# Twelve instead of sixteen weights prepared beside attention, eight converted in place in layer two, longer transfer lags in the plan, and the last product in two column halves

## The chip, the cores and the metric

One Trainium2 chip, one NeuronCore of it. The metric is the device time of one execution in microseconds (us). PE is TensorE, which multiplies; DVE is VectorE, ACT is ScalarE; POOL (GpSimd) and SP (SyncE) only issue transfers here. PSUM holds the products until ACT or DVE reads them.

## The reference

```python
scores = scale * np.matmul(q, k.transpose(0, 1, 3, 2))      # 2 batches, 12 heads, 448 tokens, 64 wide
scores = np.einsum('bhij,hg->bgij', scores, w_pre)          # mix the heads
scores = scores - np.max(scores, axis=-1, keepdims=True)
attn = np.exp(scores)
attn = attn / (np.sum(attn, axis=-1, keepdims=True) + 1e-09)
attn = np.einsum('bhij,hg->bgij', attn, w_post)             # mix them again
x = np.matmul(attn, v)                                      # -> 896 tokens x 768
h = x @ w_in;  g = h * (1.0 / (1.0 + np.exp(-1.702 * h)));  x = g @ w_out           # layer one, 768 -> 2048 -> 768
h = x @ w_in2                                                                       # layer two
P = a[0] + a[1]*h + a[2]*h*h + a[3]*h*h*h
Q = 1.0 + np.abs(b[0])*np.abs(h) + np.abs(b[1])*h*h
out = (P / (Q + 1e-06)) @ w_out2
```

The four weight matrices arrive as 64-bit words; the kernel turns each word into a 32-bit number with integer operations.

## The kernel before

**No loop sets the order.** Every piece of work is a `step` with the engines that may do it, an assumed duration, the steps it needs, a rank, and the buffers it takes and gives back. `Plan.issue` plays these steps through once while the program is built, with assumed hops between engines (`HOP`) and assumed transfer times (`DMA_LAG`, `RG_LAG`, `W_LAG`, `A_LAG`, `LD_LAG`, `ST_LAG`), and writes each engine's instructions in the order that comes out. On the chip each engine follows its list strictly and waits at each instruction for its inputs. Where a real transfer is later than assumed, the engine that needs it stands, with everything behind it in its list.

**Attention** runs over 8 chunks of query rows (4 to a batch). `scores` (L356, 6 pairs of heads to a chunk) multiplies q and k; ACT or DVE copy the pair into S; `regroup` (L392, issued by SP) sends rows of S into a tile T so that 10 query rows by 12 heads lie on 120 partitions; `pre` (L397) mixes heads; DVE takes the maximum, ACT the exponential; `post` (L446, and L449 for the last 64 keys) mixes again and turns the rows; `av` (L472) multiplies with v. There are 90 such groups; chunk 5 begins with group 57. While PE waits for the first loads, `fill` runs multiplications of a constant (L257).

**The layers.** A unit `up` (L715 to L717, 18 matmuls for one tile of 128 hidden columns and one half of 448 tokens) makes h; the activation runs on ACT and DVE; a unit `down` (L782 to L784, 12 matmuls to a half) multiplies four tiles back, and DVE adds its PSUM bank to `yt` (L271). `down` has two banks `mm`, `up` four banks `bk`. Weights and activations are split into a high and a low part, so each product takes three matmuls.

**A weight** (name: layer, u or d, number; `u` tiles 768 columns, `d` tiles 512) goes through: load of the raw words by POOL (`w_load`, L661, three `raw` buffers); ACT takes the magnitude (`wmag`, L666); DVE does four integer steps (`w_bits`, L671, L673, L675, L678); a copy gives the high part (`whi`), ACT writes its negative (`w_minus`, L700), and POOL issues an adding transfer that makes the low part (`w_part`, L692; in the plan `w`). In this kernel all 40 weights of layer two take a detour (`ahead`): they are converted early, stored to DRAM (`w_store`, L684) and fetched again (`w_fetch`, L688) when layer two needs them. The first `EARLY` = 16 of them are converted beside attention, the other 24 spread over layer one. POOL's list holds all these transfers in one row, so an adding transfer behind a load waits until that load's buffer is free.

Of the kernel before, what the change touches and what calls it, by code (L numbers as in the profile page):

```python
# [17 lines left out]
B, H, S, D = 2, 12, 448, 64  # L18
# [10 lines left out]
FQ = 4  # L29
DMA_LAG = 3500  # L30
RG_LAG = 5000
W_LAG = 4500

# [21 lines left out]
HOP |= {("pe", False): 280, ("pe", True): -80, ("pool", False): 85, ("pool", True): 100}  # L55
FILL_NS, FILL_WIN, FILL_MIN = 210, 2600, 0.55
NQ = NF // FQ
TB = 10
# [5 lines left out]
LATE = 2400, 1400, 1000  # L64
A_LAG = 5000
LD_LAG = 6500, 4500
ST_LAG = 8500, 4500
EARLY = 16
MID = 60
# [6 lines left out]
class Plan:  # L76
# [35 lines left out]
    def issue(self):  # L112
# [50 lines left out]
        while events and events[0][0] < 1e8:  # L163
# [15 lines left out]
            for e in idle:  # L179
# [23 lines left out]
                else:  # L203
                    dry.add(e)
                    if e == "pe" and self.fill and more:
                        b = next((b for b in ("bk", "mm") if self.pick(b) is not None), None)
                        if now >= self.fill_from and b and busy(now) < FILL_MIN * FILL_WIN:
                            mode = "f"
                            idle[e] = now + FILL_NS
                            runs.append((now, now + FILL_NS))  # L210
                            order.append((b, self.pick(b)))
                        heapq.heappush(events, (now + FILL_NS, 2, ()))
# [24 lines left out]
def talking_heads_then_two_ffn(ctx: ExitStack, tc: tile.TileContext, q, k, v, wpre, wpost, win1, wout1, win2, wout2, ab, out):  # L237
# [12 lines left out]
    def psum(b, *n):  # L250
        return banks[b][plan.bank[n, b]]
# [517 lines left out]

    def down(L, qq, m, halves):  # L770
        gt = t_["g", L, qq]
        p = psum("mm", "down", L, qq, m, halves)
        if m % 3 == 0:

            pe.matmul(p[:, halves[0], S:], warm[:, :128], warm[:, : 512 - S], start=True, stop=True)
        w = t_["w", (L, "d", qq * KK + m)]
        for hf in halves:
            t_["y", L, qq, m, hf] = p
            cs = slice(hf * S, hf * S + S)
            for i in range(FQ):  # L780
                ms = slice(i * 128, i * 128 + 128)
                pe.matmul(p[:, hf, :S], w[:, 0, ms], gt[:, 0, i, cs], start=i == 0, stop=False)  # L782
                pe.matmul(p[:, hf, :S], w[:, 1, ms], gt[:, 0, i, cs], start=False, stop=False)  # L783
                pe.matmul(p[:, hf, :S], w[:, 0, ms], gt[:, 1, i, cs], start=False, stop=i == FQ - 1)  # L784

    def down_out(L, qq, m, halves, eng):
        if ("yt", L) not in t_:
            t_["yt", L] = held("yt", "out", L, qq, m, halves)
        hs = slice(halves[0], halves[-1] + 1)
        o, p = t_["yt", L][:, m, hs], t_["y", L, qq, m, halves[0]][:, hs, :S]  # L790
        if qq == 0:
            cast(eng, o, p)
        else:
            add(eng, o, p, o)
# [9 lines left out]

    def store(m, halves):
        hs = slice(halves[0], halves[-1] + 1)
        sp.dma_start(out[m].rearrange("p (h s) -> p h s", h=2)[:, hs], t_["yt", 1][:, m, hs])

# [3 lines left out]
    def downs(L, qq):  # L812
        if qq < NQ - 1:
            return [("down", L, qq, m, both) for m in range(KK)]
        if L == 0:
            return [("down", L, qq, m, (hf,)) for hf in range(2) for m in range(KK)]
        return [("down", L, qq, m, both) for m in range(KK - 1)] + [("down", L, qq, KK - 1, (hf,)) for hf in range(2)]

# [16 lines left out]

    ahead = sorted((k_ for k_ in uses if k_[0] == 1), key=lambda k_: rank[uses[k_][0]])

# [40 lines left out]
    for L in range(2):  # L878
        for ft in range(NF):
            qq = ft // FQ  # L880
            for hf in range(2):
# [8 lines left out]
                for i in range(parts):  # L890
                    if L == 0:
                        d0 += [("xlo", ci, a) for ci in chunks_of[hf] for a in range(2) if 3 * a < (i + 1) * KK // parts]
                    if L == 1:
                        d0 += [("xn", kk, hf) for kk in range(i * KK // parts, (i + 1) * KK // parts)]
                    name = u if i == parts - 1 else u + (i,)
                    step(name, "pe", 3700 // parts, d0, p, up, L, ft, hf, i, parts, take=[] if i else ["bk"])
                    d0 = [name]
# [26 lines left out]
        for qq in range(NQ):  # L924
            for u in downs(L, qq):
                _, _, _, m, halves = u
                p = rank[u]
                d0 = [("g", L, qq * FQ + i, hf) for i in range(FQ) for hf in halves]
                d0.append(("w", (L, "d", qq * KK + m)))
                step(u, "pe", 2465 * len(halves), d0, p, down, L, qq, m, halves, take=["mm"])  # L930
                o = ("out",) + u[1:]
                lead = u == first_out
                d0 = [] if lead else [("out",) + first_out[1:]]
                if qq:
                    d0 = [("out", L, qq - 1, m, both)]
                n = len(halves) * S
                ways = joining(n, "out") if qq else copying(n, "first", True)
                step(o, ways, 0, [u] + d0, p + RANK["out"], down_out, L, qq, m, halves, None, take=["yt"] if lead else [], give=[("mm", u)])
                if qq == NQ - 1 and L == 0:
# [6 lines left out]
                elif qq == NQ - 1:  # L946
                    step(("st", m) + halves, "sp", 640, [o], p, store, m, halves)
            mark(("gend", L, qq), [u for u in downs(L, qq)], [("g", ("ghi", L, qq * FQ, 0))])
# [69 lines left out]
```

## Time and profile before

| | |
|---|---|
| time, median of 3 runs | 710.62 us (709.89 to 711.29) |
| the profiled execution | 710.44 us, of which its span is 708.6 us |
| PE busy | 699.1 us, 99% of the span |
| DVE, ACT, POOL busy | 518.2, 458.7, 235.2 us |
| share of the chain that ended last | PE 82%, DMA 7%, DVE 4% |

The span reaches from the first to the last instruction. Attention lasts to about 223 us, layer one to 470, layer two to the end.

### The profile page before, as it was taken

Reading aid. Unit: us, or ns where it says so; the run is one execution under the profiler, and the core shown is the slowest. Engines: PE = TensorE matmul, PEld = TensorE weight load, DVE = VectorE, ACT = ScalarE, POOL = GpSimd, SP = SyncE. Lnnn points to the kernel's source line nnn. Section 1 sums busy time; section 2 is a strip of 40 time slices with the busy share of each in tenths; the row PEclk is TensorE's granted clock in tenths of the full one; section 3 lists DMA queues with packets and bytes.
Section 4 is the critical chain, followed back from the end, with each engine's and each line's share of the span. In section 5 each row is a group of like instructions: output and inputs, shape, how many; then the busy total and the mean of one; then the engine's idle time right before and its main releaser. Section 6 shows DMA issues by size and latency. Waiting matters only on the chain.

```text
span 708.6 us, 11989 instructions
## 1 busy us (share of the span) xinstructions
PE 699.1 (99%) x4304; PEld 596.3 (84%) x4304; DVE 518.2 (73%) x1105; ACT 458.7 (65%) x863; POOL 235.2 (33%) x377
## 2 busy tenths in 40 slices
PE   9999999999999999999999999999999999999997
PEld 5686767776778899999999898899999999999997
DVE  4688768776797697877777778949997287588522
ACT  4878676768796566665654454659987677476420
POOL 0412122211223465656465355522221222221120
PEclk9999999999999999999999999999999999999999
DMA  6886777746464588899977878874644565541263
GB/s 213 242 274 216 235 239 240 228 171 213 166 188 148 187 237 245 265 258 253 252 207 233 229 195 247 211 173 98 149 87 106 112 140 112 142 81 31 61 156 118
DMA packets 51097, 130.34 MB, mean 184 GB/s; under 512 B 7870, under 2 KB 21758, under 8 KB 51038
## 3 DMA queue, kind: packets, MB, share of 16 engines
q0 software_dynamic: 33760, 100.16, 52.9%
q1 hardware_dynamic: 16990, 29.05, 12.5%
q8 instruction: 34, 0.56, 0.3%
q10 hardware_dynamic: 288, 0.37, 0.1%
q14 instruction: 25, 0.20, 0.1%
HBM read 71.88 MB, written 15.34 MB: 123 GB/s over the span
## 4 chain that ended last, share of the span: by engine, by line
PE 82%; DMA 7%; DVE 4%; issue 3%; ACT 2%; POOL 2%; ACTq 0%; POOLq 0%
PE bk L397 9%; PE bk L715 9%; PE bk L716 9%; PE bk L717 9%; PE mm L782 8%; PE bk L446 8%; PE mm L784 8%; PE mm L783 8%; PE bk L472 6%; PE mm L356 5%; DMA raw<-in_wout_dram 3%; DMA rawk<-in_win_dram 1%; DMA rawk<-in_wout_dram 1%; PE bk L449 1%; DMA T<-S 1%
## 5 line engine op out<-in xcount | busy, mean ns | idle before, releaser
L782 PE MATMUL mm<-g,wd 128*128 128x448 f32 x384 | 142.1, 370 | 1.2 <-DVE yt L271 1.2
L783 PE MATMUL mm<-g,wd 128*128 128x448 f32 x384 | 140.3, 365 | 0.0
L784 PE MATMUL mm<-g,wd 128*128 128x448 f32 x384 | 140.3, 365 | 0.0
L446 PEld LDWEIGHTS bk<-W,E 120*128 120x128 f32 x540 | 72.0, 191 | 33.6 <-issue 22.7
L661 POOL DMA_DIRECT2D rawk<-in_win_dram x87 | 47.5, 554 | 133.1 <-issue 35.6
L397 PE MATMUL bk<-T,wpr 120*120 120x448 f32 x180 | 82.2, 548 | 1.0 <-DMA T<-S 1.0
L782 PEld LDWEIGHTS mm<-g,wd 128*128 128x128 f32 x384 | 72.1, 188 | 7.8 <-ACT wd L700 1.2
L784 PEld LDWEIGHTS mm<-g,wd 128*128 128x128 f32 x384 | 72.1, 188 | 5.8
L783 PEld LDWEIGHTS mm<-g,wd 128*128 128x128 f32 x384 | 72.2, 188 | 5.6 <-DMA wd<-wm 0.2
L446 PE MATMUL bk<-W,E 120*128 120x120 f32 x540 | 75.4, 277 | 0.0
L403 DVE TENSOR_REDUCE sm<-bk 120x1 f32<-120x448 f32 (+1 forms) x90 | 55.7, 621 | 26.5 <-PE bk L397 25.5
L716 PE MATMUL bk<-xh,wu 128*128 128x448 f32 x192 | 70.4, 367 | 1.4 <-DMA wu<-wm 1.4
L715 PE MATMUL bk<-xh,wu 128*128 128x448 f32 x192 | 70.6, 368 | 0.6 <-ACT t L725 0.6
L715 PE MATMUL bk<-xn,wu 128*128 128x448 f32 x192 | 70.3, 366 | 0.0
L717 PE MATMUL bk<-xh,wu 128*128 128x448 f32 x192 | 70.2, 366 | 0.0
L716 PE MATMUL bk<-xn,wu 128*128 128x448 f32 x192 | 70.1, 365 | 0.0
L717 PE MATMUL bk<-xn,wu 128*128 128x448 f32 x192 | 70.1, 365 | 0.0
L661 POOL DMA_DIRECT2D rawk<-in_wout_dram x64 | 36.7, 590 | 91.9 <-ACT E L409 35.2
L271 DVE TENSOR_TENSOR yt<-mm,yt 128x896 f32<-128x896 f32 (+1 forms) x43 | 40.1, 933 | 34.9 <-PE mm L784 34.8
L736 DVE SCALAR_TENSOR_TENSOR t<-t,cab,bk 128x448 f32<-128x448 f32 x64 | 43.4, 678 | 28.4 <-ACT t L732 17.1
L263 ACT ACTIVATE AT<-bk 128x360 f32<-128x360 f32 (+2 forms) x79 | 41.7, 531 | 27.4 <-PE bk L449 19.9
L409 ACT ACTIVATE E<-bk,sm 120x448 f32<-120x448 f32 (+1 forms) x90 | 56.3, 627 | 4.5 <-DVE sm L403 1.7
(125 smaller groups left out, 1458.5 us busy)
## 6 DMA issues: line engine op xcount, KB each, us to landing
rawk<-in_win_dram POOLq DMA_DIRECT2D x87, 256.0 KB, 4.1
T<-S SPq DMA_DIRECT2D x88, 210.0 KB
rawk<-in_wout_dram POOLq DMA_DIRECT2D x64, 256.0 KB, 4.7
raw<-in_wout_dram POOLq DMA_DIRECT2D x32, 256.0 KB, 5.3
d1u<-wmk POOLq DMA_DIRECT2D x22, 192.0 KB, 5.8
rawk<-d1d POOLq DMA_DIRECT2D x16, 256.0 KB, 3.1
wd<-rawk POOLq DMA_DIRECT2D x16, 256.0 KB, 3.4
d1d<-wmk POOLq DMA_DIRECT2D x15, 256.0 KB, 5.8
```

What stands on the lines that cost most here:

```text
L397: pe.matmul(p[:K, :S], wpr[:K, :K], t_["T", t][:K], start=True, stop=True)
L403: dve.tensor_reduce(t_["sm", t][:K, 0:1], t_["pre", t][:K, :S], AX.X, ALU.max, negate=True)
L409: act.activation(t_["E", t][:K], t_["pre", t][:K, :S], AF.Exp, bias=sm[:K, 0:1], scale=1.0, accum_out=sm[:K, 1:2])
L446: pe.matmul(o, t_["E", t][:K, jc * 128 : jc * 128 + 128], t_["W", t][:K], start=True, stop=True)
L661: pool.dma_start(r[:, c : c + 256], src[:, c : c + 256])
L715: pe.matmul(p[:, :S], w[:, 0, ws], x[:, 0, kk], start=kk == 0, stop=False)
L716: pe.matmul(p[:, :S], w[:, 1, ws], x[:, 0, kk], start=False, stop=False)
L717: pe.matmul(p[:, :S], w[:, 0, ws], x[:, 1, kk], start=False, stop=kk == KK - 1)
L736: dve.scalar_tensor_tensor(t, t, col(i), t_[("h",) + key][:, :S], ALU.add, ALU.mult)
L782: pe.matmul(p[:, hf, :S], w[:, 0, ms], gt[:, 0, i, cs], start=i == 0, stop=False)
L783: pe.matmul(p[:, hf, :S], w[:, 1, ms], gt[:, 0, i, cs], start=False, stop=False)
L784: pe.matmul(p[:, hf, :S], w[:, 0, ms], gt[:, 1, i, cs], start=False, stop=i == FQ - 1)
```

## The change

- `EARLY` 12 instead of 16: four weights less are converted beside attention.
- `AHEAD` = 32: the last eight weights of layer two (d 16 to d 23) take no detour; they are loaded, converted and split in layer two itself, without store and fetch. 20 weights instead of 24 are spread over layer one.
- Assumed transfer times: `W_LAG` 4500 to 5200, `A_LAG` 5000 to 6500, the second entries of `LD_LAG` and `ST_LAG` 4500 to 5200 (all ns). Assumed durations: `up` 3700 to 3650, a half `down` 2465 to 2435.
- A filling pair is assumed to take twice as long in the first 6 us (`FILL_COLD`).
- The last `down` of layer two (m = 5, second half) is cut into two halves of 224 columns, each with its own bank, addition and store.

```diff
-W_LAG = 4500
+W_LAG = 5200
...
+FILL_COLD = 6000
...
-A_LAG = 5000
-LD_LAG = 6500, 4500
-ST_LAG = 8500, 4500
-EARLY = 16
+A_LAG = 6500
+LD_LAG = 6500, 5200
+ST_LAG = 8500, 5200
+EARLY = 12
+AHEAD = 32
...
-                            idle[e] = now + FILL_NS
-                            runs.append((now, now + FILL_NS))
+                            ns = FILL_NS * (2 if now < FILL_COLD else 1)
+                            idle[e] = now + ns
+                            runs.append((now, now + ns))
...
+    def columns(hf, cut):
+        n = S if cut is None else S // 2
+        c = hf * S + (cut or 0) * n
+        return slice(c, c + n), n
...
-                pe.matmul(p[:, hf, :S], w[:, 0, ms], gt[:, 0, i, cs], start=i == 0, stop=False)
+                pe.matmul(p[:, hf, :n], w[:, 0, ms], gt[:, 0, i, cs], start=i == 0, stop=False)
...
-        return [("down", L, qq, m, both) for m in range(KK - 1)] + [("down", L, qq, KK - 1, (hf,)) for hf in range(2)]
+        return [("down", L, qq, m, both) for m in range(KK - 1)] + [("down", L, qq, KK - 1, (0,))] + [("down", L, qq, KK - 1, (1,), c) for c in range(2)]
...
-    ahead = sorted((k_ for k_ in uses if k_[0] == 1), key=lambda k_: rank[uses[k_][0]])
+    ahead = sorted((k_ for k_ in uses if k_[0] == 1), key=lambda k_: rank[uses[k_][0]])[:AHEAD]
...
-                    step(name, "pe", 3700 // parts, d0, p, up, L, ft, hf, i, parts, take=[] if i else ["bk"])
+                    step(name, "pe", 3650 // parts, d0, p, up, L, ft, hf, i, parts, take=[] if i else ["bk"])
...
-                step(u, "pe", 2465 * len(halves), d0, p, down, L, qq, m, halves, take=["mm"])
+                step(u, "pe", 2435 * len(halves) // (1 + len(cut)), d0, p, down, L, qq, m, halves, *cut, take=["mm"])
```

In the changed kernel lines stand three further down in attention and in the weight steps (L397 is L400, L661 is L664, L692 is L695, L271 is L274).

**PE, attention, between chunk 5's scores and its first `pre`.** Rows in PE's list; the `pre` of T_1527 (before) and T_1487 (changed) is the first of chunk 5, group 57, and waits for a regroup of S that needs all of chunk 5's scores. Before:

```order
L446 MATMUL bk_67<-W_1505,E_1474 128x120 x3
L397 MATMUL bk_68<-T_1259,wpr 120x448
L446 MATMUL bk_69<-W_1521,E_1497 128x120 x3
L449 MATMUL bk_69<-wsrc,R_1508 128x120
L397 MATMUL bk_67<-T_1276,wpr 120x448
L446 MATMUL bk_66<-W_1556,E_1525 128x120 x3
L397 MATMUL bk_69<-T_1293,wpr 120x448
L397 MATMUL bk_68<-T_1328,wpr 120x448
L446 MATMUL bk_66<-W_1573,E_1547 128x120 x3
L449 MATMUL bk_66<-wsrc,R_1558 128x120
L446 MATMUL bk_67<-W_1590,E_1566 128x120 x3
L397 MATMUL bk_69<-T_1527,wpr 120x448
```

Changed:

```order
L449 MATMUL bk_67<-W_1504,E_1489 128x120 x3
L452 MATMUL bk_67<-wsrc,R_1481 128x120
L400 MATMUL bk_66<-T_1255,wpr 120x448
L400 MATMUL bk_69<-T_1268,wpr 120x448
L400 MATMUL bk_67<-T_1284,wpr 120x448
L449 MATMUL bk_68<-W_1543,E_1514 128x120 x3
L359 MATMUL mm_64<-k_879,q_1093 120x448 x2
L359 MATMUL mm_65<-k_879,q_1093 120x448 x2
L449 MATMUL bk_66<-W_1550,E_1526 128x120 x3
L452 MATMUL bk_66<-wsrc,R_1548 128x120
L449 MATMUL bk_68<-W_1573,E_1540 128x120 x3
L400 MATMUL bk_69<-T_1487,wpr 120x448
```

Counted from chunk 5's last scores to that `pre`, PE's list held 5 groups of `pre`, 6 of `post` and 3 additions to it (L449); now it holds 7, 7 and 3, and two pairs of scores of chunk 6 besides.

**POOL, layer one, around weight u 13.** Its adding transfer is `wu<-wm_2622` before and `wu<-wmk_84` in the changed kernel. Before:

```order
L661 DMA rawk_82<-in_wout_dram 128x512 x2
L684 DMA d1d_3802<-wm_2621 128x512
L661 DMA rawk_81<-in_win_dram 128x512 x3
L661 DMA raw_2620<-in_wout_dram 128x512 x2
L692 DMA wu<-wm_2622 128x768
L692 DMA wd_2626<-wm_2623 128x512
```

Changed:

```order
L664 DMA raw_2588<-in_wout_dram 128x512 x2
L695 DMA wd_2595<-wmk_83 128x512
L664 DMA rawk_81<-in_win_dram 128x512 x3
L695 DMA wu<-wmk_84 128x768
L664 DMA rawk_82<-in_win_dram 128x512 x3
L687 DMA d1u_3691<-wm_2589 128x384 x2
```

Two loads stood directly ahead of it; now one does, and the second follows it.

**DVE, the end of layer one.** The two additions of 896 columns are those of `down` (0, 2, 4) and (0, 2, 5), the one of 448 columns is the first of the half units. Before:

```order
L271 TENSOR_TENSOR yt_2619<-mm_64,yt_2619 128x896
L678 SCALAR_TENSOR_TENSOR wmk_83<-rawk_81,wmk_83 128x512
L671 TENSOR_SCALAR wmk_84<-wmk_84 128x512
L673 TENSOR_SCALAR wmk_84<-wmk_84 128x512
L675 SCALAR_TENSOR_TENSOR wmk_84<-raw_2620,wmk_84 128x512
L678 SCALAR_TENSOR_TENSOR wmk_84<-raw_2620,wmk_84 128x512
L265 CAST wd_2627<-wmk_83 128x512
L271 TENSOR_TENSOR yt_2619<-mm_65,yt_2619 128x896
L671 TENSOR_SCALAR wm_2621<-wm_2621 128x512
L673 TENSOR_SCALAR wm_2621<-wm_2621 128x512
L675 SCALAR_TENSOR_TENSOR wm_2621<-rawk_82,wm_2621 128x512
L271 TENSOR_TENSOR yt_2619<-mm_64,yt_2619 128x448
```

Changed:

```order
L274 TENSOR_TENSOR yt_2587<-mm_64,yt_2587 128x896
L676 TENSOR_SCALAR wmk_84<-wmk_84 128x768
L678 SCALAR_TENSOR_TENSOR wmk_84<-rawk_81,wmk_84 128x768
L681 SCALAR_TENSOR_TENSOR wmk_84<-rawk_81,wmk_84 128x768
L674 TENSOR_SCALAR wm_2589<-wm_2589 128x512
L676 TENSOR_SCALAR wm_2589<-wm_2589 128x512
L678 SCALAR_TENSOR_TENSOR wm_2589<-rawk_82,wm_2589 128x512
L274 TENSOR_TENSOR yt_2587<-mm_65,yt_2587 128x896
L681 SCALAR_TENSOR_TENSOR wm_2589<-rawk_82,wm_2589 128x512
L674 TENSOR_SCALAR wm_2590<-wm_2590 128x512
L676 TENSOR_SCALAR wm_2590<-wm_2590 128x512
L274 TENSOR_TENSOR yt_2587<-mm_64,yt_2587 128x448
```

Before, weight d 21 (`wmk_84`) had all its four integer steps ahead of the second addition; now three of them (`wm_2589`) stand there and the last follows. Behind these rows, from the first half unit's addition to that of the seventh, DVE's list holds 16 integer steps and a cast before, and 14 and none now.

## Rows read from the trace of the kernel before

**Rows 1.** The page's first line.

```profile
span 708.6 us, 11989 instructions
```

**Rows 2.** Waits of PE: us in total, times, longest.

```profile
PE bk L716 <- DMA wu<-wm: 1.4, 1, 1.4
...
PE mm L782 <- DVE yt L271: 1.2, 2, 0.9
PE bk L397 <- DMA T<-S: 1.0, 1, 1.0
PE bk L715 <- ACT t L725: 0.6, 1, 0.6
```

**Rows 3.** Timeline of PE, 1 to 9 us: start, duration, instructions, count.

```profile
1.17 3.77 PE L257 MATMUL bk<-warm 128*128 128x240 f32 x16 [1.17 <-DVE warm L276]
4.87 2.31 PE L356 MATMUL mm<-k,q 64*120 64x448 f32 x8
7.01 1.67 PE L362 MATMUL bk<-k,q 64*120 64x448 f32 x8
```

**Rows 4.** DMA, 0 to 12 us, in 40 slices of 0.3 us.

```profile
GB/s 0 0 0 0 0 24 111 100 282 392 375 398 395 400 392 384 376 335 341 358 388 413 353 374 328 305 347 202 19 29 10 0 0 0 0 0 0 163 86 173
```

**Rows 5.** Chain that ended last, 128 to 148 us: start, us, what.

```profile
129.61 1.70 PE mm L356 x8
...
132.25 0.66 PE bk L446 x6
132.91 0.75 PE bk L397 x2
...
134.66 1.73 ACT S L263 x2
...
136.41 8.42 DMA T<-S
```

**Rows 6.** Timelines of ACT and DVE, 233 to 237 us.

```profile
233.92 1.28 ACT L725 ACT_TABLE_LOAD   x1 [1.71 <-PE bk L472]
...
236.07 0.43 DVE L268 TENSOR_TENSOR xh<-bk,xh 128x264 fp32r<-128x264 f32 x1 [3.40 <-ACT xh L263]
```

**Rows 7.** Timeline of POOL, 382 to 388 us.

```profile
383.08 1.59 POOL L661 DMA_DIRECT2D rawk<-in_win_dram  x3 [4.75 <-issue]
385.33 1.07 POOL L661 DMA_DIRECT2D raw<-in_wout_dram  x2 [0.66 <-ACT wm L666]
386.39 0.94 POOL L692 DMA_DIRECT2D wu<-wm  x1
```

**Rows 8.** Chain that ended last, 429 to 446 us.

```profile
432.57 4.90 DMA raw<-in_wout_dram
...
440.95 1.00 DVE yt L271
...
442.33 0.44 DVE wm L673
...
442.79 0.69 DVE wm L675
```

**Rows 9.** Stretches: PE, PEld, DVE, ACT, POOL busy (instructions), granted clock, DMA share, GB/s.

```profile
438.30:470.00 31.70, 30.53 (x151) 27.26 (x149) 26.20 (x49) 16.86 (x27) 15.48 (x22) 1.00 0.84 221
648.30:670.30 22.00, 22.00 (x111) 20.40 (x110) 15.53 (x26) 11.36 (x20) 3.75 (x5) 1.00 0.25 48
706.00:707.00 1.00, 0.00 (x0) 0.00 (x0) 0.00 (x0) 0.00 (x0) 0.00 (x0) 1.00 0.62 229
```

**Rows 10.** The page's DMA issues: count, KB, median us to landing.

```profile
raw<-in_wout_dram POOLq DMA_DIRECT2D x32, 256.0 KB, 5.3
...
wd<-wm POOLq DMA_DIRECT2D x14, 256.0 KB, 5.9
```

**Rows 11.** Timelines of PE and DVE, 699 to 705 us.

```profile
699.66 0.37 PE L782 MATMUL mm<-g,wd 128*128 128x448 f32 x1
...
702.10 0.36 PE L782 MATMUL mm<-g,wd 128*128 128x448 f32 x1
...
704.73 0.62 DVE L271 TENSOR_TENSOR yt<-mm,yt 128x448 f32<-128x448 f32 x1 [1.81 <-PE mm L784]
```

More of the change, by code (lines that the diff above doesn't have):

```diff
@@ L768, in g_part, with down @@
             cast(eng, gt[:, 0, i, cs], src)
-    def down(L, qq, m, halves):
+    def columns(hf, cut):
+        n = S if cut is None else S // 2
+        c = hf * S + (cut or 0) * n
+        return slice(c, c + n), n
+    def down(L, qq, m, halves, cut=None):
         gt = t_["g", L, qq]
-        p = psum("mm", "down", L, qq, m, halves)
+        p = psum("mm", "down", L, qq, m, halves, *([] if cut is None else [cut]))
         if m % 3 == 0:
@@ L777, in down, with down_out @@
         for hf in halves:
-            t_["y", L, qq, m, hf] = p
-            cs = slice(hf * S, hf * S + S)
+            t_["y", L, qq, m, hf, cut] = p
+            cs, n = columns(hf, cut)
             for i in range(FQ):
                 ms = slice(i * 128, i * 128 + 128)
-                pe.matmul(p[:, hf, :S], w[:, 0, ms], gt[:, 0, i, cs], start=i == 0, stop=False)
-                pe.matmul(p[:, hf, :S], w[:, 1, ms], gt[:, 0, i, cs], start=False, stop=False)
-                pe.matmul(p[:, hf, :S], w[:, 0, ms], gt[:, 1, i, cs], start=False, stop=i == FQ - 1)
-    def down_out(L, qq, m, halves, eng):
+                pe.matmul(p[:, hf, :n], w[:, 0, ms], gt[:, 0, i, cs], start=i == 0, stop=False)
+                pe.matmul(p[:, hf, :n], w[:, 1, ms], gt[:, 0, i, cs], start=False, stop=False)
+                pe.matmul(p[:, hf, :n], w[:, 0, ms], gt[:, 1, i, cs], start=False, stop=i == FQ - 1)
+    def down_out(L, qq, m, halves, *rest):
+        cut, eng = rest if len(rest) > 1 else (None, *rest)
         if ("yt", L) not in t_:
@@ L789, in down_out @@
         hs = slice(halves[0], halves[-1] + 1)
-        o, p = t_["yt", L][:, m, hs], t_["y", L, qq, m, halves[0]][:, hs, :S]
+        cs, n = columns(0, cut)
+        o, p = t_["yt", L][:, m, hs, cs], t_["y", L, qq, m, halves[0], cut][:, hs, :n]
         if qq == 0:
@@ L803, in xn_part, with store @@
             cast(eng, x[:, 0, m], s_)
-    def store(m, halves):
+    def store(m, halves, cut=None):
         hs = slice(halves[0], halves[-1] + 1)
-        sp.dma_start(out[m].rearrange("p (h s) -> p h s", h=2)[:, hs], t_["yt", 1][:, m, hs])
+        cs, _ = columns(0, cut)
+        sp.dma_start(out[m].rearrange("p (h s) -> p h s", h=2)[:, hs, cs], t_["yt", 1][:, m, hs, cs])
     both = (0, 1)
@@ L925, in talking_heads_then_two_ffn @@
             for u in downs(L, qq):
-                _, _, _, m, halves = u
+                m, halves, *cut = u[3:]
                 p = rank[u]
@@ L935, in talking_heads_then_two_ffn @@
                     d0 = [("out", L, qq - 1, m, both)]
-                n = len(halves) * S
+                n = len(halves) * S // (1 + len(cut))
                 ways = joining(n, "out") if qq else copying(n, "first", True)
-                step(o, ways, 0, [u] + d0, p + RANK["out"], down_out, L, qq, m, halves, None, take=["yt"] if lead else [], give=[("mm", u)])
+                step(o, ways, 0, [u] + d0, p + RANK["out"], down_out, L, qq, m, halves, *cut, None, take=["yt"] if lead else [], give=[("mm", u)])
                 if qq == NQ - 1 and L == 0:
@@ L946, in talking_heads_then_two_ffn @@
                 elif qq == NQ - 1:
-                    step(("st", m) + halves, "sp", 640, [o], p, store, m, halves)
+                    step(("st", m) + halves + tuple(cut), "sp", 640, [o], p, store, m, halves, *cut)
             mark(("gend", L, qq), [u for u in downs(L, qq)], [("g", ("ghi", L, qq * FQ, 0))])
```

## Prediction

> **What bounds the kernel.** I read the page's engine line first: PE is busy for 699.1 of 708.6 us [rows 1], so only time in which PE does nothing useful can be won. The rates agree: the twelve matmuls of a half unit took 702.10 - 699.66 = 2.44 us [rows 11], 0.203 us each, and between units PE's timeline shows almost no holes. Then I took PE's own waits. They are few: 1.4 us for a weight's adding transfer, 1.2 us for DVE's additions to yt, 1.0 us for a regrouped tile, 0.6 us for the first activation [rows 2]. To these come what stands ahead of the first useful matmul at 4.87 us [rows 3] and what follows the last one: DVE's final addition begins at 704.73 [rows 11], 3.9 us before the span ends. PE's arithmetic doesn't change, so the change is worth what it does to these places, less the waits that it makes elsewhere. The sum goes against this execution, 710.44 us; the median of the runs is 0.18 us above that, which I ignore. A measurement of this kernel can tell about 0.2%, 1.4 us, from no change.
>
> **Start.** Sixteen fillers took 4.87 - 1.17 = 3.70 us, 0.231 us each for 240 columns [rows 3]. That is 0.96 ns a column, against 0.45 ns in a later half unit (0.203 us for 448), so PE ran at its lower level of 1.2 GHz, although the granted clock is printed as 1.00. The eight score matmuls that follow need 2.14 us (4.87 to 7.01) and 1.70 us later on [rows 3, 5]; the 0.44 us difference is 0.88 us spent at half rate, so the higher level came at about 5.75 us. Eight fillers are gone by 1.17 + 8 x 0.231 = 3.0 us. The first scores need 344 KB of q and k (128 x 240 and 128 x 448 words); the summed slices pass 344 KB at about 3.2 us [rows 4], and with a second queue sharing the bandwidth I take 3.6. If the level still rises at 5.75, half rate does 1.07 us of work by then instead of 0.44: 0.6 us gained (0.8 if the data are there at 3.2). Against this stands the Trainium skill, "TensorE: Matmul & The Clock Gate", section "The HAM clock gate": PE starts throttled, and only sustained activity releases it. By that rule the gap between 3.0 and 3.6 may put the rise off, and by it this term would be a loss. The trace agrees that PE starts slow (0.231 us a filler); a rise put off by a gap no row here shows. By rows alone: had the rise to come as long after 3.6 as it came after 1.17 (4.6 us, so 8.2), 2.3 us of work would be done by then instead of 0.44 + 2.45 = 2.9, a loss of 0.6. PE isn't idle for long there, so I take -0.6, with +0.6 as the other end.
>
> **The regroup of chunk 5.** The chain shows it: scores end at 134.66, ACT copies for 1.73, the transfer takes 8.42 [rows 5], 10.3 us with the hops, and PE had 8.4 us of other work: 5 x 0.75 + 6 x 0.66 + 3 x 0.22 [rows 5] (the 0.22 is an estimate, a third of a post's 0.66). The changed list puts two more `pre`, one `post` and two pairs of scores there: 2 x 0.75 + 0.66 + 1.70 = 3.9 us. So the 1.0 us of [rows 2] goes, with 1.9 us to spare for a slower transfer. Chunks 6 and 7, whose scores also move ahead, gain more room. -1.0 (0 if the transfer takes 2 us longer).
>
> **Entry into layer one.** `up` (0,1) waited for the bank of `up` (0,0), held until ACT had loaded its table (1.28 us, [rows 6]) and run the first activation: 0.6 us in [rows 2]. Now its first part stands ahead of av 7, in a bank of its own. What is late next is DVE's low part of x at 236.07 + 0.43 [rows 6], which the part after that reads; some 0.2 us remain. -0.4 (0 to -0.6).
>
> **Adding transfer of u 13.** It was issued at 386.39, behind three loads' issues that had waited 4.75 us and two more from 385.33 to 386.4 [rows 7]. In POOL's new list the two-issue load is behind it, and in the order of issue the addition stands two units ahead of its use instead of one. This frees more than the 1.4 us lacking. -1.4 (0 to -1.6).
>
> **End of layer one.** Twelve half units should take 12 x 2.44 = 29.3 us; they took 31.70 [rows 9], 2.4 lost. DVE was behind: the second 896-column addition waited behind weight d 21, whose load landed 4.90 us after its issue, at 437.47, so that it came at 440.95 [rows 8], 2.65 after its product was done (438.30, where the stretch of [rows 9] begins). From there DVE's rows are as much work as PE's. The changed list takes one long step (0.69) from ahead of that addition and two integer steps and a cast, some 1.5 us at 0.44 and 0.69 each [rows 8], from the six half units behind. The longer assumed load (5200 for 4500 ns, against a median of 5.3 us, [rows 10]) puts more units between a load and its steps. I take -1.5 (0 to -2.4).
>
> **Tail.** The last unit's 24 matmuls of 224 columns are bounded by 2.44 us (no overhead) and by 24 x 0.11 = 2.64 (the post's six records of 120 columns with as wide a weight take 0.66, [rows 5]): +0.2 at most. The final addition halves from 0.62 [rows 11]: -0.25. The last store moves 0.62 us' worth of data in 706 to 707 [rows 9]; half of it: -0.25. Sum -0.3 (-0.5 to 0).
>
> **The moved conversions.** Four fewer beside attention and four fewer in layer one give DVE room; PE doesn't wait for DVE in attention [rows 2], so nothing is counted. Store and fetch of eight weights vanish from POOL's list, off the path. In layer two the eight weights' 32 integer steps, 18 us, are new. Their cover is DVE's idle time. It is thinnest between the additions of `down` (1,2,1) and (1,2,4): there DVE was busy 15.53 of 22.0 us [rows 9]; 18 of the steps stand there, 8 x 0.44 + 10 x 0.69 = 10.4, less two casts: 25 us in 22. The addition of (1,2,4) is then up to 3 us late; its bank is needed one unit (4.9 us) after its product, and an addition takes 1.0 [rows 8], so 3.9 us of lateness are free and PE waits for nothing. Without that cover each microsecond late costs one. d 18 is tighter: its copy, formerly free to start when a buffer is, now also waits for its steps, and the chain behind (copy, negative, 5.9 us of adding transfer in the worst case, [rows 10]) must end before `down` (1,3,0). I price it at 0 (bounds 0 and +3).
>
> **New waits.** PE's order in attention is rewritten at some forty places, each a chance for a wait. The old plan, with the same `RG_LAG`, left 1.6 us of waits there and at the entry. I take half: +0.8 (0 to +4).
>
> Sum: -0.6 -1.0 -0.4 -1.4 -1.5 -0.3 +0.8 = -4.4, so 710.44 - 4.4 = 706.0. All good ends and no new wait: -6.9, 703.5.
>
> **Rivals.**
> *Layer two's DVE falls behind.* If the 6.5 us in which DVE idled in that stretch were mostly waits for ACT (the activation goes back and forth) and remain, the addition is 5 or 6 us late instead of 3, PE waits some 2 us, and d 18 as much. For it: the stretch asks more than it has. Against: the integer steps fill exactly such gaps. -4.4 + 2 = 708.0.
>
> *The waits only move.* Static lists with assumed times always leave some; a list calibrated on other transfers meets others' lateness. For it: the two longest waits had loads later than assumed. Against: the assumed times now lie at or above the medians of [rows 10], where 4500 and 5000 ns lay below. New waits of 4 instead of 0.8 leave -1.2: 709.3, and with the regroup's lost too 710.
>
> *Slower: POOL's list holds additions back.* Layer one has 34 weights whose addition can stand behind a load waiting for its buffer, as u 13's did; loads come earlier in the new plan, so they wait longer for buffers, and POOL passes nothing. If six of them cost PE 1.4 us each: +8.4, which with the other terms (without u 13's) gives 716; it ends slower than before by over 1.4 us from four on. For it: 4.75 us of waiting ahead of one load [rows 7]. Against: of 34 additions only 3 now stand one unit or less ahead of their use, where 11 did.
>
> *The clock rises late.* The start costs 0.6 instead of giving it, as worked out there: -4.4 + 1.2, 707.2. For it: half the fillers. Against: PE rests for 0.6 us at most. The rule of the Trainium skill named under the start would bring it about.
>
> **The numbers.** Forecast 0.55 (its own range 703.5 to 707.5), layer two 0.17, late clock 0.05, moved waits 0.13, POOL 0.10. Faster by over 0.2% are the first three, 0.77; within 0.2% the fourth, 0.13; slower 0.10. The range begins half a microsecond under the good ends, 703.0, because PE's mix of kinds of work in attention changes as well, and ends at 711.5, which takes in the moved waits and leaves out the POOL case, 0.10, and some edges of the others.
>
> **What would show it.** First scores near 3.6 us, not 4.87; no wait of PE for T<-S near chunk 5; none for wu<-wm in layer one; the half units at the end of layer one in 30.2 us; DVE over 90% busy in the 22 us before the last `down`s without a wait of `down` for yt; the last addition 0.35 us long. It is wrong if PE's waits sum to over 4 us again, above all for wd in layer two or for T in attention.

## The result and the profile after

The changed kernel takes 704.35 us (median of 5 runs, 704.04 to 705.23) against 711.29 (709.89 to 711.98) for the kernel before on the same chip: a ratio of 0.9907, 95% interval 0.9893 to 0.9922. The profiled execution took 704.09 us, its span 702.3 us, 6.3 less than [rows 1].

PE's waits in the changed kernel, to be held against [rows 2] (the wait for `warm` is the constant that the fillers multiply, and was there before):

```profile
PE bk L260 <- DVE warm L279: 1.2, 1, 1.2
PE mm L359 <- DMA q<-in_q_dram: 0.7, 1, 0.7
PE mm L359 <- ACT S L266: 0.3, 1, 0.3
```

All four waits of [rows 2] are gone, and the only new one stands at the start (the one for S of 0.3 us is in the trace before too). PE's timeline there, as in [rows 3]:

```profile
1.17 2.06 PE L260 MATMUL bk<-warm 128*128 128x240 f32 x8 [1.17 <-DVE warm L279]
3.96 3.35 PE L359 MATMUL mm<-k,q 64*120 64x448 f32 x8 [0.73 <-DMA q<-in_q_dram]
7.10 2.06 PE L365 MATMUL bk<-k,q 64*120 64x448 f32 x8
8.99 1.67 PE L359 MATMUL mm<-k,q 64*120 64x448 f32 x8
```

The first sixteen score multiplications began 0.91 us earlier than before, but the seventeenth began at 8.99, and in the trace before at 8.52:

```profile
8.52 1.67 PE L356 MATMUL mm<-k,q 64*120 64x448 f32 x8
```

So the start became worse. Stretches of the changed kernel, columns as in [rows 9]: one microsecond of the start, the half units at the end of layer one, and the 22 us of layer two where the moved conversions are thickest:

```profile
5.00:6.00 1.00, 1.00 (x6) 0.52 (x4) 0.00 (x0) 0.14 (x1) 0.00 (x0) 1.00 0.98 330
...
434.47:464.10 29.63, 29.63 (x151) 27.49 (x149) 23.40 (x42) 17.43 (x28) 13.91 (x21) 1.00 0.82 198
642.40:664.40 22.00, 22.00 (x111) 20.40 (x110) 21.99 (x41) 14.15 (x26) 5.98 (x9) 1.00 0.36 98
```

The half units took 29.63 us where they had taken 31.70 [rows 9]. In that stretch of layer two DVE was busy for 21.99 of 22 us, and PE did not wait once in the layer.

Where the 6.3 us came from is read by following the same multiplication through both traces. Each row gives its start, and the last column what the stretch since the row above gained or lost:

| the same place in both programs | before | changed | gap | stretch |
|---|---|---|---|---|
| seventeenth score multiplication | 8.52 | 8.99 | +0.47 | +0.47 |
| layer one, the 31st multiplication of `up` (all `av` are done) | 237.15 | 235.57 | -1.58 | -2.05 |
| first `down` | 268.18 | 266.00 | -2.18 | -0.60 |
| `up` (0,13), second half | 395.60 | 391.77 | -3.83 | -1.65 |
| first half unit | 438.30 | 434.47 | -3.83 | 0.00 |
| first `up` of layer two | 470.00 | 464.10 | -5.90 | -2.07 |
| last half unit | 702.10 | 696.20 | -5.90 | 0.00 |
| end of the span | 708.6 | 702.3 | -6.3 | -0.4 |

### The profile page after: what moved, and what is told of

Same layout as the page of the kernel before. It is cut to its first block, busy times and chain, and to the rows that moved or that the text cites. A ratio compares the mean times of both kernels' runs of the same rounds, so it can differ in the third digit from the quotient of the medians.

```text
span 702.3 us, 11996 instructions
## 1 busy us (share of the span) xinstructions
PE 696.8 (99%) x4308; PEld 596.0 (85%) x4308; DVE 514.5 (73%) x1101; ACT 459.5 (65%) x868; POOL 225.6 (32%) x361
## 4 chain that ended last, share of the span: by engine, by line
PE 70%; DMA 1%; ACT 0%; DVE 0%; issue 0%; ACTq 0%
PE mm L790 11%; PE bk L718 11%; PE mm L792 11%; PE mm L791 11%; PE bk L719 11%; PE bk L720 11%; PE bk L475 1%; PE bk L449 1%; DMA rawk<-in_wout_dram 1%; PE bk L400 1%; PE bk L452 0%; ACT wmk L669 0%; PE mm L783 0%; ACT AT L266 0%; DVE yt L274 0%
## 5 line engine op out<-in xcount | busy, mean ns | idle before, releaser
L790 PE MATMUL mm<-g,wd 128*128 128x448 f32 (+1 forms) x388 | 142.5, 367 | 0.0
L792 PE MATMUL mm<-g,wd 128*128 128x448 f32 (+1 forms) x388 | 141.0, 363 | 0.0
L791 PE MATMUL mm<-g,wd 128*128 128x448 f32 (+1 forms) x388 | 140.9, 363 | 0.0
L664 POOL DMA_DIRECT2D rawk<-in_win_dram x96 | 54.6, 599 | 172.8 <-ACT E L412 34.0
L449 PEld LDWEIGHTS bk<-W,E 120*128 120x128 f32 x540 | 72.2, 191 | 33.5 <-issue 21.5
L400 PE MATMUL bk<-T,wpr 120*120 120x448 f32 x180 | 81.6, 547 | 0.1
L792 PEld LDWEIGHTS mm<-g,wd 128*128 128x128 f32 x388 | 72.9, 188 | 5.7
L790 PEld LDWEIGHTS mm<-g,wd 128*128 128x128 f32 x388 | 72.9, 188 | 5.6
L791 PEld LDWEIGHTS mm<-g,wd 128*128 128x128 f32 x388 | 73.0, 188 | 5.3
L449 PE MATMUL bk<-W,E 120*128 120x120 f32 x540 | 76.0, 277 | 0.0
L266 ACT ACTIVATE AT<-bk 128x360 f32<-128x360 f32 (+2 forms) x83 | 43.2, 527 | 26.6 <-PE bk L452 15.8
L274 DVE TENSOR_TENSOR yt<-mm,yt 128x896 f32<-128x896 f32 (+2 forms) x44 | 40.4, 919 | 27.1 <-PE mm L792 26.2
L664 POOL DMA_DIRECT2D rawk<-in_wout_dram x56 | 31.9, 595 | 74.1 <-issue 23.6
```

The costliest lines, as they stand in the source:

```text
L400: pe.matmul(p[:K, :S], wpr[:K, :K], t_["T", t][:K], start=True, stop=True)
L449: pe.matmul(o, t_["E", t][:K, jc * 128 : jc * 128 + 128], t_["W", t][:K], start=True, stop=True)
L664: pool.dma_start(r[:, c : c + 256], src[:, c : c + 256])
L790: pe.matmul(p[:, hf, :n], w[:, 0, ms], gt[:, 0, i, cs], start=i == 0, stop=False)
L791: pe.matmul(p[:, hf, :n], w[:, 1, ms], gt[:, 0, i, cs], start=False, stop=False)
L792: pe.matmul(p[:, hf, :n], w[:, 0, ms], gt[:, 1, i, cs], start=False, stop=i == FQ - 1)
```

## The experiments

### The start: twelve, sixteen, and eight again

Two kernels take the changed program and repeat some of its fillers as they are written out, so that the rest of every list stays (each `fill` writes a pair):

```diff
+        extra = 2          # 4 for sixteen fillers
         for n in order:
...
                 self.fill(*n)
+                if extra:
+                    extra -= 1
+                    self.fill(*n)
```

> The changed kernel with 12 instead of 8 filling multiplications; every other row stands as in the changed kernel. Theory: the rest of 0.73 us between the eighth filler (about 3.2 us) and the first scores (3.96) put off the rise of TensorE's rate, so that the scores ran at 0.37 us each until 7.84 instead of 5.76. Twelve fillers of 0.231 us from 1.17 end at 3.94, so there is no rest, the first scores still start at about 3.97 and the rate should rise near 5.76 again: half rate then lasts 1.8 us instead of 3.9, one microsecond less work lost, span 702.3 - 0.95 = 701.35 us. Rival: the rate rises late whatever stands there because the first scores, not the fillers, count; then the span stays at 702.3 with pairs of scores 0.74 us apart until about 7.8.

> The changed kernel with 16 filling multiplications as before the change; every other row stands as in the changed kernel. Theory: first scores at 4.87, rate rises at 5.76 as in the kernel before: the start is as before, 0.5 us better than eight fillers, span 701.8. Rival (the forecast's own term: fewer fillers gain 0.6): span 702.9.

> The changed kernel unchanged, on the same chip as the others. Theory of the start: the rate rises late again because of the rest after the eighth filler, pairs of first scores 0.74 us apart past 7 us, first useful work about 1 us behind the run with twelve fillers: span 702.3, time 704.4, some 1 us above the time with twelve. Rival: the late rise was chance of one execution; here it comes at about 5.8, span 701.4.

With twelve: 703.10 us (702.65 to 703.71), ratio to the kernel before 0.9900 (0.9882 to 0.9917), span 700.9. With sixteen: 703.68 (703.47 to 704.03), 0.9906 (0.9891 to 0.9921). The changed kernel again, on another chip: 704.47 (703.83 to 704.69), 0.9911 (0.9892 to 0.9930). The intervals overlap, so these times alone do not separate the three; the traces show where a difference comes from. PE's timeline with twelve:

```profile
1.17 2.92 PE L264 MATMUL bk<-warm 128*128 128x240 f32 x12 [1.17 <-DVE warm L283]
...
4.02 1.81 PE L363 MATMUL mm<-k,q 64*120 64x448 f32 x6
```

No rest stands behind the fillers now, the first scores begin 0.06 us later than in the changed kernel, and the sixteen are done at 7.54 instead of 8.99; 1.45 us are won and kept to the end (the first `up` starts 1.44 us earlier, the last product too). The rise itself can be worked out as the start of the scores plus twice what the sixteen took beyond 3.2 us, their time at the full rate (1.70 + 1.50). In the four traces with eight fillers (the changed kernel, its repetition, and two experiments below) that is 7.6, 8.6, 7.6 and 8.9 us; in the ten with twelve or sixteen it is never later than 6.8. So the late rise is no chance of one execution. But the rise scatters by itself: the seventeenth score multiplication begins between 7.76 and 9.03 us in the nine traces with sixteen fillers (8.52 in the middle), between 8.99 and 9.63 in the four with eight (9.25 in the middle). The 1.45 us are thus one pair of executions, and the one traced with twelve was the fastest of its four. Sixteen came out between the two, with a median 0.7 us under the changed kernel's. That twelve are better than sixteen because they end when the data land fits the trace (the scores begin at 4.02 instead of 4.87), and on the same chip their median is 0.58 us lower; the times of the two overlap. Twelve fillers are the fastest version run here, by the medians 0.2% under the changed kernel, which ran on other chips.

### Which part took the waits away

The kernel before with only the moved weights, and with only the assumed transfer times:

```diff
-EARLY = 16
+EARLY = 12
+AHEAD = 32
...
+    ahead = sorted(...)[:AHEAD]
```

> The kernel before with only the moved weights: twelve instead of sixteen beside attention, the last eight converted in layer two. Theory, that this is what took the waits away: chunk 5 has 12.3 us of work behind its scores (wait gone, -1.1), u 13's adding transfer is issued some 17 us of work ahead of its use (-1.6), and one weight's four steps instead of two weights' work stand between the additions at the end of layer one (-2): span 708.6 - 4.7 - up to 0.7 at the entry of layer one = 703.2 to 704, less than 1 us from the changed kernel once its worse start (+0.5) and its better tail (-0.4) are counted. Rival, that the longer assumed times did it: new waits for transfers in layer two or one, span 706 to 708.

```diff
-W_LAG = 4500
+W_LAG = 5200
-A_LAG = 5000
-LD_LAG = 6500, 4500
-ST_LAG = 8500, 4500
+A_LAG = 6500
+LD_LAG = 6500, 5200
+ST_LAG = 8500, 5200
```

> The kernel before with only the five longer assumed transfer times. Theory, that the moved weights and not these times took the waits away: chunk 5's first multiplication stands as close behind its scores as before (8.4 us of work), and the adding transfer of weight u 13 still stands behind a load, so 1.0 and 1.4 us of waits stay; the additions at the end of layer one still stand behind all four steps of weight d 21, at least 1 us stays: span 707.5 to 709. Rival, that the longer times did it: waits for transfers gone in layer one, 1.6 + 2.1 us less, span 705.

The moved weights alone: 706.38 us (705.43 to 708.88), ratio 0.9947 (0.9931 to 0.9964), against 0.9907 for the whole change; so some four sevenths of the gain. The profiled execution, with a span of 703.6 us, was the fastest of its six. From the first units of layer one to 659 us this trace lies within 0.2 us of the changed kernel's, so the moved weights carry the whole gain of layer one, and in attention all but 0.5 us (its start, with sixteen fillers, is 0.55 better, and PE waits once more there). One wait is left behind, in layer two, at 659.3, and the chain that ended last shows its origin:

```profile
PE mm L783 <- ACT wd L264: 0.7, 1, 0.7
```

```profile
658.20 0.54 DVE g L269
658.73 0.55 DVE t L757
659.27 0.02 issue
659.30 0.58 ACT g L264
659.88 0.53 ACT wd L264
660.41 0.44 PE mm L783
```

DVE is busy without a gap there, ACT waits for it, and the copy of a weight stands behind that on ACT. The place costs 0.9 us against the changed kernel, which has longer assumed times and also shorter assumed durations of `up` and `down`; the two were not run apart, so which of them removes it is not shown. The medians lie 2.0 us apart (on different chips), the spans of the two traces 1.3.

The longer times alone: 714.77 us (714.57 to 714.99), ratio 1.0062 (1.0048 to 1.0075), slower, where I had expected a little gain. The plan, believing in longer transfers, foresaw holes in layer one and filled them: PE's timeline holds five groups of fillers, 66 multiplications and 8.2 us, that the kernel before has not.

```profile
259.02 1.73 PE L257 MATMUL bk<-warm 128*128 128x240 f32 x14
...
285.02 1.73 PE L257 MATMUL bk<-warm 128*128 128x240 f32 x14
...
409.20 1.28 PE L257 MATMUL bk<-warm 128*128 128x240 f32 x10
```

Were these holes real? The same kernel without them (only the first eight pairs are written out):

```diff
+        fills = 0
         for n in order:
...
-                self.fill(*n)
+                fills += 1
+                if fills <= 8:
+                    self.fill(*n)
```

> The kernel before with the longer assumed transfer times, as in the earlier run, but without the 66 filling multiplications that the plan wrote into layer one; the 16 at the start stay. Theory, that these fillers were the loss and covered no real wait: PE's 8.2 us in them come back less the waits that they happened to cover, at most 0.9 us each at five places; span 713.0 - 8.2 + 0 to 4.5 = 705 to 709. Rival, that the plan's holes are real (PE would have waited there anyway): waits of some 1.7 us appear at the same five places and the span stays at 712 to 713.

714.59 us (712.73 to 716.45), ratio 1.0057 (1.0037 to 1.0077): nothing won. My theory fell: PE waits in that list when the fillers are gone, though at three places and not at five. PE's wait, and three stretches behind such waits:

```profile
PE bk L719 <- DMA wu<-wm: 6.3, 3, 2.7
```

```profile
286.50:290.00 3.50, 3.50 (x11) 3.15 (x12) 2.19 (x5) 2.36 (x3) 2.04 (x4) 0.56 0.79 272
...
337.00:342.00 5.00, 5.00 (x26) 4.54 (x25) 3.65 (x6) 1.43 (x4) 3.07 (x6) 1.00 0.91 238
...
399.00:404.00 5.00, 5.00 (x19) 4.46 (x18) 4.82 (x9) 2.85 (x5) 2.82 (x5) 0.66 0.49 172
```

The waits are 6.3 us for adding transfers, the transfers that I had named under the slower rival. Each was issued right behind a load on POOL, but the transfers themselves took 6.6 to 7.6 us (median of ten in the trace before: 5.1), so POOL's list is only a part of it. After the rests of 2.69 and 2.06 us the granted clock of the next stretch was 0.56 and 0.66 (a mean over both levels), and eleven multiplications filled 3.5 us where seventeen would; after the one of 1.55 us it stayed at 1.00. So the fillers cover real waits and keep the clock as well: in the trace with them the clock's mean over the span was 1.000, without them 0.994.

Last of this group, sixteen weights beside attention as before, eight converted in layer two:

```diff
 EARLY = 16
+AHEAD = 32
...
+    ahead = sorted(...)[:AHEAD]
```

> The kernel before with the last eight weights of layer two converted there, but still sixteen beside attention (so sixteen instead of twenty-four or twenty in layer one). Theory: layer one's waits go because its lists carry fewer conversions, u 13's adding transfer stands some 27 us of work ahead of its use: no wait in layer one, the half units in 29.4 us, and at most 1 us of waits in layer two as in the run with the moved weights alone. Chunk 5 keeps 8.4 us of work behind its scores, so a wait of 0 to 1.1 us there, as the two traces of the kernel before have it, and the entry wait of 0.7 stays. Span 703.5 to 705.5. Rival, that the fewer weights beside attention made the gain: waits in layer one stay, span 707 or more.

712.15 us (710.57 to 714.40), ratio 1.0018 (1.0003 to 1.0032). The sum was wrong by 6 us, though both old waits of layer one did go: measured against the kernel before, the stretch over `up` (0,13) gained 1.66 us and the end of layer one 2.07 (29.63 instead of 31.70). The loss is one new place, seen in the chain:

```profile
364.91 1.07 POOL rawk L662 x2
365.98 6.41 DMA wu<-wm
372.39 0.02 issue
...
372.49 0.67 ACT wm L667
373.16 0.02 issue
373.18 0.43 DVE wm L672
...
374.39 1.10 DVE yt L272
```

An adding transfer took 6.41 us; ACT needed its buffer for the next weight's magnitude, DVE's first integer step of that weight waited for ACT, and DVE's addition stood behind the step. PE rested 2.58 us and then ran at a granted clock of 0.51 (375.6 to 379.0): 4.4 us in all, against the kernel before. The plan of this kernel assumes 5.0 us for such a transfer, the changed one 6.5. That the longer value would have put the step behind the addition fits this, but it wasn't run by itself, and the kernel with only the moved weights assumes 5.0 too and has no such wait. So taking weights out of layer one isn't enough by itself, even with fewer left there (sixteen) than in the changed kernel (twenty). Twelve beside attention without the eight in layer two was not run.

### Single waits, moved by hand

Here the lists of the kernel before stay as planned except for one or two rows. In the first kernel the load of d 17 goes behind the adding transfer of u 13 on POOL, and four steps of d 21 go behind an addition on DVE (`behind(last, *moved)` puts steps right behind `last`):

```diff
...
+        behind(("w", (0, "u", 13)), ("eld", (1, "d", 17)))
+        behind(("out", 0, 2, 5, (0, 1)), *[("wb", (0, "d", 21), i) for i in range(4)])
         for n in order:
```

> The kernel before with its lists as planned, but two moves by hand: on POOL the two-issue load of weight d 17 goes behind the adding transfer of u 13, and on DVE the four integer steps of weight d 21 go behind the second 896-column addition at the end of layer one. Nothing else moves, no work is added or removed. Theory (waiting behind a late load is what costs): the adding transfer goes out at 384.7 instead of 386.4, PE's 1.4 us wait for it goes, -1.4 to -1.6; the addition comes at about 438.4 instead of 440.9, PE's 0.9 us wait at 441 goes, but DVE has as much work as PE from there, so only the 0.86 us that it stood idle are won: -0.9. Sum -2.4, span 706.2. Rival (the waits are set by total load on POOL and DVE, not by what stands ahead): the waits come back one or two units later, under 0.8 us won in the two places together, span 708 or more.

The second move is not to be read: the load of d 23 uses the buffer of d 21's words and now stood ahead of these steps, so they worked on d 23's words and waited for them (PE 3.8 us). It also makes the whole 715.30 us (712.91 to 716.52; 1.0060, 1.0041 to 1.0079). What comes before that place can be read. PE's waits from 395 to 434 us:

```profile
PE mm L790 <- DVE yt L279: 0.9, 1, 0.9
PE bk L724 <- DMA wu<-wm: 0.4, 1, 0.4
```

The wait for u 13 went, 1.40 us, and waits came back soon: 0.4 for u 14's adding transfer at 413, 0.9 for an addition at 431. At 433 us nothing was left of the 1.40 (the gap to the kernel before: -1.25 us ahead of u 13, -2.65 behind it, -0.92 at 433). This is one trace, and executions differ: the next kernel's trace, without this move, has 0.56 us at the same addition, which neither trace of the kernel before has.

The second kernel moves the addition alone, ahead of d 21's steps:

```diff
+        out = ("out", 0, 2, 5, (0, 1))
+        order.remove(out)
+        order.insert(order.index(("wb", (0, "d", 21), 0)), out)
```

> The kernel before with one move by hand at the end of layer one: the second 896-column addition on DVE goes ahead of the four integer steps of weight d 21 and the copy of d 20; nothing is added or removed. Theory, that the late load of d 21 held the addition: it comes some 2 us earlier, and PE's 0.9 us wait at about 441 goes; DVE stands idle there for 0.86 us and is else as busy as PE, so of the 2.4 us lost in the twelve half units at most 0.9 to 1.1 are won, and the wait near 451 may grow. Rival, that DVE's total work behind the addition sets the end: the half units still take over 31.4 us, under 0.3 us won.

710.70 us (709.22 to 712.21), ratio 0.9992 (0.9977 to 1.0007): nothing. PE's waits from 425 to 470 us in this kernel and, in the second fence, in the repetition of the kernel before:

```profile
PE mm L786 <- DMA wd<-wm: 1.1, 2, 0.7
PE mm L785 <- DVE yt L274: 0.8, 2, 0.6
```

> The kernel before unchanged, for a second trace. Question one: in the first trace the units of layer one from 237 to 264 us ran 2% slower (1.24 instead of 1.215 us for six multiplications), worth 0.6 us. Theory: this belongs to the kernel's order (what DVE and ACT do beside it) and shows again; rival: it belongs to that one execution and is absent or elsewhere. Question two: do the waits for u 13, chunk 5 and the additions show again with the same lengths (1.4, 1.0, 1.2 us within 0.3)? Ratio to before 1.000 within 0.002.

```profile
PE mm L782 <- DVE yt L271: 1.2, 2, 0.9
PE mm L783 <- DMA wd<-wm: 0.5, 2, 0.3
```

The 0.9 us wait became one of 0.6 at another addition, and the weights' adding transfers, which the additions had covered, are now waited for twice as long. The twelve half units took 32.00 us, in the repetition 32.35 and in the first trace 31.70; the rival had said over 31.4. It holds: what stood ahead of this one row did not set the end of layer one.

The repetition itself gave 710.36 us (708.82 to 712.94), ratio 0.9996 (0.9982 to 1.0010). Its trace has no wait at chunk 5; PE reached layer one 1.44 us earlier, 0.76 of them from an earlier rise of the clock at the start. But then it waited 1.84 instead of 1.41 us for u 13 and also longer at the end of layer one, so that of 1.91 us at `up` (0,4) 0.96 was left at the end. The 2% slower stretch was absent (question one): six multiplications took 1.215 us.

### How far it goes, and the tail

Sixteen instead of eight weights converted in layer two (`AHEAD = 24` in the changed kernel):

> The changed kernel with sixteen instead of eight weights converted in layer two. Theory, that DVE and the adding transfers are the limit there: the plan itself foresees three holes and writes 32 filling multiplications (0.124 us each, 4.0 us) into layer two, and the chip needs about that: span 702.4 + 4 = 706.4, 705 to 710. Rival, that layer two has room to spare: PE waits nowhere there and the loss is just the fillers, 706.4, with the adding transfers landing well before PE has done the fillers.

712.16 us (710.76 to 713.87), ratio 1.0015 (1.0001 to 1.0029). PE did the 32 fillers and waited beside them:

```profile
PE mm L791 <- DMA wd<-wm: 1.8, 2, 1.5
PE mm L791 <- DMA wd<-wmk: 1.4, 1, 1.4
...
PE bk L719 <- DMA wu<-wm: 1.0, 1, 1.0
```

Against the changed kernel 8.9 us are lost, all between 637 and 679 us: twice what the plan foresaw (by the medians 7.8, on different chips). Eight fit into layer two's late stretch and sixteen do not; nothing between was run.

The changed kernel with the last product whole:

```diff
-... + [("down", L, qq, KK - 1, (0,))] + [("down", L, qq, KK - 1, (1,), c) for c in range(2)]
+... + [("down", L, qq, KK - 1, (hf,)) for hf in range(2)]
```

> The changed kernel with its last product whole, as before the change (448 columns, one addition, one store); everything else in the same order. Theory: the cut costs PE 0.2 us in more and shorter multiplications and gives back 0.6 behind the last one; from the start of the last half unit to the end of the span 6.5 us here against 6.1, so the span is 0.4 us longer, not more than a measurement of the time can tell. Rival: the last store's fixed time sets the end and the cut only adds PE time: 0.2 us shorter without it.

704.23 us (704.05 to 705.63), ratio 0.9910 (0.9890 to 0.9929), no difference that the time shows. The last additions, whole and (second fence) cut:

```profile
698.60 0.62 DVE L274 TENSOR_TENSOR yt<-mm,yt 128x448 f32<-128x448 f32 x1 [1.81 <-PE mm L792]
```

```profile
699.07 0.39 DVE L274 TENSOR_TENSOR yt<-mm,yt 128x224 f32<-128x224 f32 x1 [0.95 <-PE mm L792]
```

From the start of the last half unit to the end it is 6.43 us whole (695.97 to 702.4) and 6.10 cut (696.20 to 702.3): the cut gives 0.33 us.

## Why the prediction was right, and where it was not

The forecast was 706.0, the range 703.0 to 711.5; it came out 1.65 us lower than forecast, and the direction was right. The two profiled executions lie 6.3 us apart, where the sum has 4.4. Term by term, from the table of the same multiplications:

- **Start, forecast -0.6, came +0.47.** This is the step that failed outright. I let the rise stay at 5.75 us because PE would rest for 0.6 us at most. It rested 0.73, and the pairs of scores ran at 0.74 us until 7.84: the bound of +0.6 was nearly met, and the rival of the late clock was right in its mechanism, though its time, 707.2, was missed for other reasons. The +0.47 is one pair of traces; between the middle ones of nine and four traces it is +0.7. The rule of the Trainium skill, "TensorE: Matmul & The Clock Gate", section "The HAM clock gate", that only sustained activity releases the throttle, agrees with the traces: four with the rest are late, and the one with twelve fillers, which has no rest, is early.
- **Attention, entry and new waits, forecast -1.0 - 0.4 + 0.8 = -0.6, came -2.05.** The two waits went as described, and no new one came; +0.8 was too much. But chunk 5's wait belonged to that one execution: the four other traces in which PE has the same list of attention (the repetition, the two moves by hand, and the kernel with sixteen weights beside attention) don't have it, and this stretch takes 227.5 to 227.9 us there instead of 228.63. In the six traces with the changed kernel's list it takes 226.3 to 226.7. So 0.9 to 1.6 us of the 2.05 are gained from execution to execution; the rest, some 0.7 to 1.1, is the bad luck of the execution that I forecast from. What the part beyond the entry wait comes from is not shown.
- **First units of layer one, not in the forecast, -0.60.** In the profiled execution six multiplications took 1.24 us up to 264 us, in the changed kernel 1.215. Four of the five traces whose list has the 0.6 us wait at the entry run so, none of the nine others. What causes it stays open; the granted clock is printed as 1.00 in both.
- **u 13, forecast -1.4, came -1.65; end of layer one, -1.5, came -2.07.** The sizes hold, the reasons only in part. I put each down to one row that stood ahead of another; the moves by hand show that undoing just that gives nothing that lasts, other waits come instead. I also called DVE's rows at the end of layer one as much work as PE's, but by [rows 9] DVE was busy for 26.20 of the 31.70 us and PE for 30.53. The moved weights are what took both waits away: with them alone PE waits for nothing in layer one. The number of weights left there doesn't explain it by itself: with 24 there are waits, with 20 none, but with 16 (and sixteen beside attention) both old waits are gone and a new one costs 4.4 us. That loads and adding transfers set the pace there, and that PE's wait is only where their lateness shows, fits the waits seen but is argued, not shown.
- **Longer assumed times.** I had counted them as a help at the end of layer one and against the rival of the moved waits. By themselves they made the kernel slower by 0.6%; beside the moved weights they are, together with the shorter assumed durations, worth about 0.9 us, in layer two.
- **Layer two, forecast 0, came 0.00.** DVE was busy for 21.99 of 22 us, more than the 90% named as the sign, and the addition of (1,2,4) was 1.3 us late (665.71 against 664.4), inside the 3.9 that were free. The rival is near: without the longer times and the shorter durations 0.9 us are lost there, with eight more weights 8.9.
- **Tail, forecast -0.3, came -0.4;** measured by itself 0.33.
- **The slower rival** (POOL's list holds additions back) did not come true in the changed kernel: PE waits for no adding transfer. With the longer times alone PE waited 6.3 us for such transfers once the fillers were out of the way; these transfers stood behind loads but also took 6.6 to 7.6 us, and the two causes were not separated.

The terms were further off than the sum. The start came 1.07 us worse than forecast; better came attention with the new waits (1.45), the first units of layer one (0.60), the end of layer one (0.57), u 13 (0.25) and the tail (0.1). Together that is 1.9 us, and that it is not 3.0 is luck: the error at the start hid a third of the others. The direction doesn't hang on this luck.

## What to carry to other kernels

In a program whose order is fixed ahead, a wait in the profile shows where lateness ends, and not always where it begins: move the row by hand first, and if waits turn up again a few units later, the row that stood ahead was not the cause. Taking work away helped here when four weights left layer one and four left attention, and not when eight left layer one alone, so the new list has to be run and its waits read again. Work moved into an engine's idle time is free until that time is used up: with eight weights DVE was busy for all but 0.01 us of the fullest stretch, with sixteen PE waited. Raising the assumed times without taking work away made a plan here that expects waits instead of one that avoids them. And a wait that a forecast is to win back should be in more than one trace.

Before fillers are taken away at a cold start, look when the first data land: PE should have something to multiply until then.

## What the runs showed of the hardware

- The granted clock is printed as 1.00 for 5 to 6 us of the changed kernel, while pairs of scores there took 0.74 us instead of 0.37: at the start the lower level (1.2 GHz) shows in the durations alone. In mid-program it does show: 0.51 to 0.66 in the stretches behind rests of 2.06, 2.58 and 2.69 us. Behind the rests of 1.46, 1.55 and 1.84 us it stayed at 1.00.
- So a wait of 2.7 us cost far more than itself: behind it multiplications took 0.37 us each instead of 0.20 for some 3.4 us.
- At the cold start the rise comes at a different time in each execution: with sixteen fillers and the same rows, the seventeenth score multiplication began anywhere from 7.76 to 9.03 us.
- On the chip of the result five runs of the kernel before spread over 2.1 us and five of the changed kernel over 1.2. That a list without waits passes on less of the transfers' scatter fits this, but was not tested.
